# Norms transposed in pairs inside the projections of a two-layer transformer block, and four smaller moves

## The chip, the cores and the metric

The kernel runs on one core of a Trainium2 chip. The metric is the time of one execution on the device in microseconds. The engines are TensorE (PE: matmuls and transposes; PEld: its weight loads), VectorE (DVE), ScalarE (ACT), GpSimd (POOL) and SyncE (SP, which here only issues DMAs). DMAs are issued by SP, by ScalarE and by GpSimd, each in its own queue.

## What is computed

Two layers, with the same weights, over x of 2048 rows by 512 columns, all in float32:

```python
for _ in range(2):
    x = x + attention(layernorm(x), wqkv, wo)      # 32 heads of 16
    x = x + mish_mlp(layernorm(x), w1, b1, w2)     # 512 -> 1792 -> 512

# attention: softmax(q @ k.T * 16 ** -0.5) @ v, heads joined, then @ wo
# mish_mlp:  h = n @ w1 + b1;  (h * tanh(softplus(h))) @ w2
```

## The kernel before, in words

**Precision.** Every matmul of weights and activations is done as three: each operand is split into a high part, a rounded copy, and a low part, the difference, and `mm3` (L157) adds high x high, high x low and low x high. A projection step over 512 contraction rows is 4 blocks (k = 0 to 3) of 3 matmuls, 12 in all. `split_psum` (L153) splits a PSUM accumulator: ScalarE writes the high part, VectorE subtracts it from the accumulator for the low part. `split_load` (L109) loads a weight block; its inner `split` has ScalarE write the high part and GpSimd the low part.

**Stages of a layer.** The rows are cut into NCH = 4 chunks of 512; a chunk is 4 tiles of 128 rows.

1. Norm of each chunk (`norm_parts`, L164, a generator that gives the work out in parts): statistics of 4 tiles on VectorE (L175, L176), the power -1/2 on GpSimd (L172), the normalized tile `xn` on VectorE (L188), 4 transposes on TensorE (L199) for each tile, and the split into `th` and `tl` (L200). A chunk's `th` and `tl` are needed whole by the first projection step that reads it.
2. Projections (`qkv`, L446): a list `order` of steps (m, c), m = 0 to 3 for q and 4 to 7 for k, c the chunk. Each step accumulates in one of three PSUM accumulators (tag "s"), is split into a tile `pt` and written by a DMA that ScalarE issues (L479) to a scratch tensor `scr[m]` in DRAM. Once the eight steps with m in (0, 4) are done, `prep_qk(0)` reads the q and k rows of the first head group back: 2 pairs u by 2 heads e, each 7 transfers (one of ones, three of k, three of q), 28 in all, e = 0 on SP and e = 1 on GpSimd (L248). Later steps are followed by the first row maxima (`some_max`). Then v is projected (`v_parts`, L500).
3. Attention (`Attention.run`, L395), the longest stage: an order of scores, maxima and products written out by hand. It is not touched.
4. Output projection (`wo_parts`, called as `project`, L727). Between its blocks of three matmuls, the parts of the first norm for the hidden layer are placed by a table of block numbers (L741).
5. Hidden layer (`mlp`, L589): for each chunk c and each of FT = 14 blocks f, `hid` does the matmuls, ScalarE and VectorE the mish, with two products on GpSimd (L608, L611), and `outp`, two blocks later, the second matmul. The norms of the following chunk, and in layer 0 the norms of chunks 0 to 2 for layer 1, are spread over its blocks (`spread`, L207). The last norm for layer 1 is done inside `qkv` when chunk 3 is first needed (`late`, L462).

**What sets the order.** The kernel is written in program order; a planner then orders each engine's instructions by its own estimate of when each is ready, with three exceptions. `behind` (L100) pins an instruction behind the one written before it on the same engine. `att.pe` (L228) chains TensorE instructions in the order written, but only when `att.chained` is set, before the change only after `prep_qk(0)` (L489). DMA queues and engines then run in the order planned, each instruction waiting in its turn.

**Buffers.** Tag "f" has 2 buffers of 512 columns; it holds `xn`, the mish's `hb` and the attention's output tile `ot`. Tag "raw" has 3 buffers of 1024 columns; it holds raw weights and every second `pt`. Tag "ah" has 2, for the mish. Tag "mx" has 2 pairs of PSUM banks.

**Before the projections of layer 0**, L666 to L677 load chunk 0 of x, two weight blocks and the other chunks, and write out the norms of all four chunks; the planner mixes their transposes among the first steps.

Of the kernel before, what the change touches and what calls it, by code (L numbers as in the profile page):

```python
# [18 lines left out]
P = 128  # L19
S, D, H, DH, F = 2048, 512, 32, 16, 1792  # L20
NCH = 4
# [21 lines left out]
KEEP = 2  # L43
GSTEPS = NCH * NKT
# [9 lines left out]
def kernel(ctx: ExitStack, tc: tile.TileContext, x, wqkv, wo, w1, b1, w2, out):  # L54
# [20 lines left out]
    nc.sync.dma_start(b1t, b1.rearrange("(f p) -> p f", p=P))  # L75
# [33 lines left out]
    def split_load(key, src, a, b, later, raw=None):  # L109
        t = b8([P, 2, a, b], F32R, "s" + key)  # L110
        if raw is None:
            raw = tmp.tile([P, a, b], F32, tag="raw", name="r" + key, bufs=3)
        behind(nc.sync.dma_start(raw, src))

        def split():
            behind(nc.scalar.activation(t[:, 0], raw, AF.Copy))
            behind(nc.gpsimd.tensor_tensor(t[:, 1], raw, t[:, 0].bitcast(F32), op=ALU.subtract))
            unkept.append((key, t))

        later.append(split)  # L120
        return t
# [42 lines left out]
    def norm_parts(src, nm, got, key, tag, fine=False, pin=lambda ins: ins, pe=lambda ins: ins, halves=False):  # L164
# [20 lines left out]
        for t in range(NCH):  # L185
            xn = t512("f", f"xn{nm}{t}")
            pin(
                nc.vector.tensor_scalar(  # L188
                    xn, src[:, t], mv[:, t, 0:1], rs[:, t : t + 1], op0=ALU.subtract, op1=ALU.mult
                )  # L190
            )
            if halves:
                yield
            if tag == "mx":
                tp = ps.tile([P, 2, 512], F32, tag=tag, name=f"tp{nm}{t}")[:, 0]
            else:
                tp = pbank(tag, f"tp{nm}{t}")
            for k in range(KT):
                pe(nc.tensor.transpose(tp[:, ts(k, P)], xn[:, ts(k, P)], ident))  # L199
# [3 lines left out]
    def norm(src, nm, got, key, tag, fine=False):  # L203
        for _ in norm_parts(src, nm, got, key, tag, fine):
            pass
# [6 lines left out]
    class Attention:  # L212
# [26 lines left out]
        def prep_qk(self, g):  # L239
            l = self.l  # L240
            ks, qs = [], []
            for u in range(HG // 2):
# [3 lines left out]
                for e in range(2):  # L246
                    r0 = e * HALF
                    queue = nc.gpsimd if g == 0 and e else nc.sync  # L248
                    queue.dma_start(
                        k[r0 + KROWS : r0 + MROWS].bitcast(F32).rearrange("p (r n) -> p r n", n=P),  # L250
                        ones[:, None, :].to_broadcast([MROWS - KROWS, S // P, P]),
                    )
                    yield
                    for t, parts, base in ((k, K_PARTS, NCH), (q, Q_PARTS, 0)):
                        for j, a in enumerate(parts):
                            queue.dma_start(
                                t[r0 + j * DH : r0 + (j + 1) * DH].bitcast(F32),
                                self.scr[base + m][a, (h0 + e) * DH : (h0 + e + 1) * DH, :].bitcast(F32),
                            )
                            yield  # L260
# [172 lines left out]
    def load_qkv(l, wts, which, later):  # L433
        raw = None
        for j in which:
# [3 lines left out]
            elif j < 4:  # L439
                wts[j] = split_load(key, *cols(wqkv, j), later)  # L440
# [5 lines left out]
    def qkv(l, wts, tt, order, late, due):  # L446
        scr = [dram.tile([2, P, S], F32R, name=f"scr{l}{m}") for m in range(2 * NCH)]
        att = Attention(l, scr)
# [10 lines left out]
        spare = []  # L459
        for n, (m, c) in enumerate(order):  # L460
            if c not in tt:
                late()  # L462
# [6 lines left out]
            else:  # L469
# [3 lines left out]
            mm3(  # L473
                acc,
                [(w[:, 0, k, ts(m % 2, P)], w[:, 1, k, ts(m % 2, P)], th[:, k], tl[:, k]) for k in range(KT)],
                pe=att.pe,
            )
# [4 lines left out]
            for fn in due.get((m, c), []):  # L482
                fn()
            if m in (0, 4):
                done += 1
                if done == 2 * NCH:
                    for _ in att.prep_qk(0):
                        pass
                    att.chained = True  # L489
# [8 lines left out]
        return att  # L498
# [90 lines left out]
    def mlp(l, x2s, w1t, w2t, tts, dst, hooks):  # L589
        acts, obs = {}, {}  # L590

        def hid(c, f):
# [15 lines left out]
            nc.gpsimd.tensor_tensor(hb, hb, e, op=ALU.mult)  # L608
            ah, al = t512("ah", "ah" + nm, F32R), t512("al", "al" + nm, F32R)
            nc.vector.tensor_tensor(ah, hb, r, op=ALU.mult)  # L610
            nc.gpsimd.tensor_tensor(hb, hb, r, op=ALU.mult)  # L611
# [43 lines left out]
    wts, tt, late = {}, {}, None  # L655
# [11 lines left out]
    load_qkv(0, wts, (0, 2), splits)  # L667
    xc.append(load_x(1))
    for c in range(NCH):
        parts = norm_parts(xc[c], f"q0{c}", tt, c, "mx", c == 0)  # L670
        next(parts)
        if c == 0:
            split_all(splits)
        for _ in parts:
            pass
        if c + 2 < NCH:
            xc.append(load_x(c + 2))  # L677
    for l in range(2):
        due = {}
        if l == 0:  # L680
# [8 lines left out]
        att = qkv(l, wts, tt, order, late, due)  # L689
# [90 lines left out]
        if l == 0:  # L780
            late = lambda: norm(x2s[last], f"q1{last}", tt, last, "mx", True)
# [29 lines left out]
```

## Time and profile before

| | |
|---|---|
| time of the runs, median of 3 (lowest to highest) | 3623.95 us (3623.9 to 3626.84) |
| the profiled execution's own time | 3625.2 us |
| its span, first to last instruction | 3623.4 us |
| mean granted TensorE clock | 0.997 |
| attention, layer 0 (100 to 1455 us, with the end of its projections): TensorE busy | 1345.1 of 1355 us |
| attention, layer 1 (1900 to 3258 us): TensorE busy | 1347.8 of 1358 us |

Lines of a profile name an engine, a line of the kernel (L199), an operation and the tiles it writes and reads, as out<-in. In a view in order of time, a line begins with start and duration in microseconds, "x4" joins four instructions, and the bracket says how long the engine stood idle before and who released it. In a view of waits, a line has the waiting instruction, the one it waited for, and total, number and longest in microseconds. "ACTq" or "SPq" is a DMA being issued on that engine's queue.

### The profile page before, as it was taken

How to read it: one execution, taken by the hardware profiler on the slowest of the kernel's cores; microseconds unless marked ns; L12 is line 12 of the kernel's file. 1: busy time of each engine (PE TensorE's matmuls, PEld its weight loads, DVE VectorE, ACT ScalarE, POOL GpSimd, SP SyncE). 2: the span in 40 equal slices, each digit the busy share in tenths (PEclk: the TensorE clock that was granted, in tenths of full speed). 3: DMA queues.
4: the chain of work that ended last, by engine and by line, in shares of the span. 5: the costliest groups of instructions: out<-in, count | busy, mean ns of one | idle time of the engine just before them, and what ended most of it. 6: DMA issues, size and time to landing. Idle time of an engine off the chain costs nothing. (4 is left out here: it accounts for less than half of the span.)

```text
span 3623.4 us, 69472 instructions
## 1 busy us (share of the span) xinstructions
PE 3553.0 (98%) x28784; PEld 1948.5 (54%) x28784; DVE 2963.7 (82%) x2978; ACT 2520.7 (70%) x3475; POOL 567.6 (16%) x589
## 2 busy tenths in 40 slices
PE   7999999999999999999999999999999999999999
PEld 5644444444444444777776444444444444447887
DVE  4779999999999994666647799999999999946565
ACT  2178888888888888344421788888888888873444
POOL 2200101001000002345421000000000000024455
PEclk9999999999999999999999999999999999999999
DMA  6551313313122224600164311112021211245000
GB/s 192 202 157 38 79 49 69 68 40 78 48 51 60 51 78 65 183 35 12 47 197 150 66 31 35 36 40 43 19 46 28 46 33 33 78 69 179 36 12 24
DMA packets 128707, 254.07 MB, mean 70 GB/s; under 512 B 18680, under 2 KB 62584, under 8 KB 114568
## 3 DMA queue, kind: packets, MB, share of 16 engines
q1 hardware_dynamic: 101896, 174.58, 19.8%
q0 software_dynamic: 8224, 35.21, 3.5%
q10 hardware_dynamic: 18272, 39.85, 3.0%
q8 instruction: 226, 3.70, 0.4%
q14 instruction: 89, 0.73, 0.1%
HBM read 148.38 MB, written 99.09 MB: 68 GB/s over the span
## 5 line engine op out<-in xcount | busy, mean ns | idle before, releaser
L297 DVE TENSOR_REDUCE mxv<-pm 128x2 f32<-128x1024 f32 x2048 | 2388.0, 1219 | 180.7 <-PE pm L293 132.7
L348 ACT ACTIVATE p<-sp 128x1024 f32<-128x1024 f32 x1366 | 1396.9, 1023 | 17.5 <-PE sp L347 12.3
L373 PE MATMUL pv<-p,va 128*32 128x128 f32 (+3 forms) x16048 | 1166.9, 392 | 0.0
L293 PE MATMUL pm<-ks,qs 48*128 48x512 f32 x4096 | 1106.8, 445 | 0.2
L358 ACT ACTIVATE p<-ss 128x512 f32<-128x512 f32 x1364 | 815.2, 598 | 384.7 <-PE ss L357 290.3
L347 PE MATMUL sp<-qs,ks 50*128 50x512 f32 x2732 | 737.8, 447 | 4.5 <-ACT p L348 2.2
L293 PEld LDWEIGHTS pm<-ks,qs 48*128 48x128 f32 x4096 | 460.0, 184 | 360.6 <-issue 256.8
L373 PEld LDWEIGHTS pv<-p,va 128*32 128x32 f32 x16048 | 368.2, 108 | 498.2 <-issue 417.8
L357 PE MATMUL ss<-qs,ks 50*128 50x512 f32 x1364 | 610.7, 448 | 0.1
L357 PEld LDWEIGHTS ss<-qs,ks 50*128 50x128 f32 x1364 | 252.0, 185 | 305.3 <-ACT p L358 210.6
L347 PEld LDWEIGHTS sp<-qs,ks 50*128 50x128 f32 x2732 | 276.7, 183 | 202.3 <-ACT p L348 117.3
L320 POOL CAST np<-nf 16x128 fp32r<-16x128 f32 x64 | 17.9, 280 | 2230.5 <-ACT nf L319 2188.2
L608 POOL TENSOR_TENSOR hb<-hb,he 128x512 f32<-128x512 f32 x112 | 157.6, 1407 | 188.2 <-DVE he L605 184.1
L611 POOL TENSOR_TENSOR hb<-hb,hr 128x512 f32<-128x512 f32 x112 | 160.4, 1432 | 137.3 <-DVE ah L610 129.5
L612 DVE TENSOR_TENSOR al<-hb,ah 128x512 fp32r<-128x512 f32 x112 | 108.0, 964 | 84.5 <-POOL hb L611 82.2
L606 ACT ACTIVATE hr<-he 128x512 f32<-128x512 f32 x112 | 70.8, 632 | 151.6 <-POOL hb L611 77.0
L154 ACT ACTIVATE pt<-qk 128x512 fp32r<-128x512 f32 x64 | 37.9, 598 | 158.9 <-PE qk L162 127.5
L604 ACT ACTIVATE he<-he 128x512 f32<-128x512 f32 x112 | 70.8, 632 | 102.9 <-DVE he L603 99.7
L602 ACT ACTIVATE hb<-h,b1t 128x512 f32<-128x512 f32 x112 | 76.8, 685 | 77.2 <-DVE al L612 52.0
L610 DVE TENSOR_TENSOR ah<-hb,hr 128x512 fp32r<-128x512 f32 x112 | 76.9, 687 | 61.4 <-ACT hr L607 34.3
L605 DVE SCALAR_TENSOR_TENSOR he<-he 128x512 f32<-128x512 f32 x112 | 79.9, 714 | 41.9 <-ACT he L604 39.1
L603 DVE TENSOR_SCALAR he<-hb 128x512 f32<-128x512 f32 x112 | 68.0, 608 | 48.5 <-POOL hb L608 33.9
(225 smaller groups left out, 3277.7 us busy)
## 6 DMA issues: line engine op xcount, KB each, us to landing
scr<-pt ACTq DMA_DIRECT2D x64, 512.0 KB
qs<-scr SPq DMA_DIRECT2D x180, 128.0 KB
ks<-scr SPq DMA_DIRECT2D x180, 128.0 KB
vscr<-v SPq DMA_DIRECT2D x32, 512.0 KB
va<-vscr SPq DMA_DIRECT2D x64, 256.0 KB
oscr<-ot SPq DMA_DIRECT2D x64, 256.0 KB
ww<-sw POOLq DMA_DIRECT2D x14, 1024.0 KB, 5.2
qs<-np SPq DMA_DIRECT2D x512, 2.0 KB
```

The source lines that it names most:

```text
L293: nc.tensor.matmul(pm[:, e], qs[u][rows, q0 : q0 + P], ks[u][rows, ts(n, 512)], start=True, stop=True)
L297: nc.vector.tensor_reduce(self.mxs[b][:, 2 * u : 2 * u + 2, qt, n], pm, axis=AX.X, op=ALU.max)
L347: self.pe(nc.tensor.matmul(sp[:, e], k, q, start=True, stop=True))
L348: nc.scalar.activation(self.pts[-1][:, 0:n], sp[:, 0:n], AF.Exp, scale=SCALE)
L357: self.pe(nc.tensor.matmul(sp, k, q, start=True, stop=True))
L358: nc.scalar.activation(self.pts[i // 3][:, 2], sp, AF.Exp, scale=SCALE)
L373: nc.tensor.matmul(self.accs[b][ts(h, VW), cols], self.va[b // NCH][:, kt, h, :], self.pts[j][:, e, cols], start=kt == 0 and q0 == 0, stop ...
L605: nc.vector.scalar_tensor_tensor(e, e, 2.0, e, op0=ALU.add, op1=ALU.mult)
L608: nc.gpsimd.tensor_tensor(hb, hb, e, op=ALU.mult)
L610: nc.vector.tensor_tensor(ah, hb, r, op=ALU.mult)
L611: nc.gpsimd.tensor_tensor(hb, hb, r, op=ALU.mult)
L612: nc.vector.tensor_tensor(al, hb, ah.bitcast(F32), op=ALU.subtract)
```

## The change

1. `norm_parts` for tag "mx": four `xn` are made at once, in buffers of "f" and "ah"; two tiles are transposed into both banks of a pair, and split by one ScalarE and one VectorE instruction of 1024 columns. These norms are pinned (`behind`) and chained (`att.pe`).
2. `qkv` takes a table `within`: at block k of step n it goes on with a norm. In layer 0 the statistics and `xn` of chunks 1, 2, 3 are written at the start of steps 0, 3, 6, their transposes before blocks 1 and 3 of steps 2, 5, 7. In layer 1 the last norm's parts stand at step 4 and at blocks 0 and 2 of step 9, and the step (5, 1) is moved ahead of (0, 3). `att.chained` is set from the first instruction on.
3. `prep_qk(0)`: the 14 transfers of the second pair (u = 1) are issued by ScalarE, pinned, two after each later step; of the first pair 7 are on SP and 7 on GpSimd.
4. The low halves of the first two weight blocks are formed by VectorE, not GpSimd. The load of the bias b1 moves from the head of SP's queue behind the loads of x.
5. Norms spread over the hidden layer (tag "acc") take `xn` from "raw" instead of "f". The table of block numbers in the output projections changes. In the last two blocks of the last chunk, the mish's two products are done by VectorE instead of GpSimd.

```diff
+PREP = 7
...
-    def split_load(key, src, a, b, later, raw=None):
+    def split_load(key, src, a, b, later, raw=None, low=nc.gpsimd):
...
-            behind(nc.gpsimd.tensor_tensor(t[:, 1], raw, t[:, 0].bitcast(F32), op=ALU.subtract))
+            behind(low.tensor_tensor(t[:, 1], raw, t[:, 0].bitcast(F32), op=ALU.subtract))
...
-        for t in range(NCH):
-            xn = t512("f", f"xn{nm}{t}")
+        def scaled(t, tag):
+            if tag == "raw":
+                xn = tmp.tile([P, 2, 512], F32, tag=tag, name=f"xn{nm}{t}", bufs=3)[:, 0]
+            else:
+                xn = t512(tag, f"xn{nm}{t}")
...
+        if tag == "mx":
+            xns = [scaled(t, ("f", "ah")[t // 2]) for t in range(NCH)]
+            yield
+            for u in range(NCH // 2):
+                tp = ps.tile([P, 2, 512], F32, tag=tag, name=f"tp{nm}{u}")
+                for e in range(2):
+                    for k in range(KT):
+                        pe(nc.tensor.transpose(tp[:, e, ts(k, P)], xns[2 * u + e][:, ts(k, P)], ident))
+                two = ts(u, 2 * P)
+                split_psum(
+                    th[:, :, two].rearrange("p k (t n) -> p k t n", n=P),
+                    tl[:, :, two].rearrange("p k (t n) -> p k t n", n=P),
+                    tp.rearrange("p t (k n) -> p k t n", n=P),
+                    pin,
+                )
+                yield
+            return
+        for t in range(NCH):
+            xn = scaled(t, "raw" if tag == "acc" else "f")
...
-                    queue = nc.gpsimd if g == 0 and e else nc.sync
+                    queue = nc.sync
+                    pin = lambda ins: ins
+                    if g == 0 and u:
+                        queue, pin = nc.scalar, behind
+                    elif g == 0 and e:
+                        queue = nc.gpsimd
...
-            if c not in tt:
-                late()
+            for fn in within.get((n, 0), []):
+                fn()
...
+            for k in range(KT):
+                for fn in within.get((n, k), []) if k else []:
+                    fn()
+                mm3(
+                    acc,
+                    [(w[:, 0, k, ts(m % 2, P)], w[:, 1, k, ts(m % 2, P)], th[:, k], tl[:, k])],
+                    first=k == 0,
+                    last=k == KT - 1,
+                    pe=att.pe,
+                )
...
+            for _ in range(2):
+                next(parts, None)
             if m in (0, 4):
                 done += 1
                 if done == 2 * NCH:
-                    for _ in att.prep_qk(0):
-                        pass
-                    att.chained = True
+                    parts = att.prep_qk(0)
+                    for _ in range(2 * PREP):
+                        next(parts)
...
-            nc.gpsimd.tensor_tensor(hb, hb, e, op=ALU.mult)
+            mul = nc.vector if (l, c) == (1, NCH - 1) and f >= FT - 2 else nc.gpsimd
+            mul.tensor_tensor(hb, hb, e, op=ALU.mult)
...
-            nc.gpsimd.tensor_tensor(hb, hb, r, op=ALU.mult)
+            mul.tensor_tensor(hb, hb, r, op=ALU.mult)
...
-    load_qkv(0, wts, (0, 2), splits)
-    xc.append(load_x(1))
-    for c in range(NCH):
-        parts = norm_parts(xc[c], f"q0{c}", tt, c, "mx", c == 0)
...
+    load_qkv(0, wts, (0, 2), splits, nc.vector)
+    xc += [load_x(c) for c in range(1, NCH)]
+    nc.sync.dma_start(b1t, b1.rearrange("(f p) -> p f", p=P))
+    att = attention(0)
+    att.chained = True
+    norms = [norm_parts(xc[c], f"q0{c}", tt, c, "mx", c == 0, behind, att.pe) for c in range(NCH)]
+    for i in range(4):
+        next(norms[0])
+        if i > 1:
+            splits.pop(0)()
...
+            for c, (n0, n1) in enumerate(((0, 2), (3, 5), (6, 7)), 1):
+                for at in ((n0, 0), (n0, 0), (n1, 1), (n1, 3)):
+                    within.setdefault(at, []).append(lambda c=c: next(norms[c]))
...
-            order = [(0, 0), (0, 1), (0, 2), (4, 0), (4, 1), (4, 2), (1, 0), (1, 1), (1, 2), (5, 0), (0, 3), (4, 3)]
+            order = [(0, 0), (0, 1), (0, 2), (4, 0), (4, 1), (4, 2), (1, 0), (1, 1), (1, 2), (5, 0), (5, 1), (0, 3), (4, 3)]
+            att = attention(1)
+            att.chained = True
+            late = norm_parts(x2s[NCH - 1], f"q1{NCH - 1}", tt, NCH - 1, "mx", True, pe=att.pe)
+            for at in ((4, 0), (4, 0), (9, 0), (9, 2)):
+                within.setdefault(at, []).append(lambda: next(late))
...
-            for n in range({0: 1, 6: 1, 9: 2, 12: 2, 15: 2}.get(i, 0)):
+            for n in range({0: 1, 8: 1, 11: 2, 14: 2}.get(i, 0)):
                 next(first)
         for i, _ in enumerate(project(2)):
-            if i == 1:
+            for n in range({1: 2, 4: 1}.get(i, 0)):
                 next(first)
```

More of the change, by code (lines that the diff above doesn't have):

```diff
@@ L431, in run, with load_qkv @@
             open_banks()
-    def load_qkv(l, wts, which, later):
+    def load_qkv(l, wts, which, later, low=nc.gpsimd):
         raw = None
@@ L439, in load_qkv @@
             elif j < 4:
[L440 removed]
+                wts[j] = split_load(key, *cols(wqkv, j), later, low=low)
             else:
```

47 lines of the change are left out of this document (14 added, 33 removed).

## The prediction

> **What bounds the kernel now.** I read the page's head first, then busy time by stage (columns: stage, its length, then busy us and instructions of TensorE, its weight loads, VectorE, ScalarE, GpSimd; granted clock; DMA).
>
> ```profile
> span 3623.4 us, 69472 instructions
> PE 3553.0 (98%) x28784; PEld 1948.5 (54%) x28784; DVE 2963.7 (82%) x2978; ACT 2520.7 (70%) x3475; POOL 567.6 (16%) x589
> ```
>
> ```profile
> 8.83:100.00 91.17, 76.84 (x325) 61.12 (x326) 44.04 (x83) 26.45 (x43) 25.63 (x26) 0.94 0.65 208
> 1455.00:1482.00 27.00, 25.86 (x146) 18.67 (x145) 19.68 (x33) 3.00 (x5) 4.22 (x5) 1.00 0.67 186
> 1482.00:1750.00 268.00, 264.37 (x1177) 215.34 (x1176) 169.16 (x250) 121.62 (x188) 133.50 (x102) 1.00 0.17 58
> 1750.00:1832.00 82.00, 77.01 (x347) 59.70 (x345) 49.57 (x86) 39.21 (x63) 33.38 (x26) 1.00 0.23 84
> 1832.00:1900.00 68.00, 62.00 (x258) 50.12 (x260) 24.59 (x46) 13.96 (x25) 13.78 (x21) 0.92 0.70 211
> 3258.00:3282.00 24.00, 21.36 (x124) 15.42 (x121) 17.23 (x27) 2.99 (x5) 2.94 (x2) 1.00 0.67 177
> 3282.00:3612.00 330.00, 327.93 (x1461) 268.82 (x1460) 199.12 (x290) 152.37 (x235) 166.70 (x125) 1.00 0.15 53
> 3612.00:3618.50 6.50, 4.80 (x19) 2.99 (x17) 2.33 (x4) 1.35 (x2) 2.58 (x2) 1.00 0.00 0
> ```
>
> TensorE sets the time, so a change that leaves its work alone can win only its idle time and its time at a lower clock. Its idle time here is 14.3 us in the first projections, 6.0 in the second ones, 3.6, 5.0 and 2.1 in the hidden layers, 1.1 and 2.6 in the output projections, 1.7 at the tail: 36 us. At full clock a matmul costs 327.93/1461 = 0.225 us, so one step of the projections (12 matmuls) 2.7 us. Next I asked whom TensorE waits for (total, times, longest): the first five lines are from 8 to 100 us, the next three from 1832 to 1900, the last two from 1750 to 1832.
>
> ```profile
> PE tpq L199 <- DVE xnq L188: 8.8, 1, 8.8
> PE tpq L199 <- DVE tlq L155: 6.6, 3, 5.1
> PE qk L160 <- DVE pt L155: 4.0, 2, 3.1
> PE tpq L199 <- DVE mvq L176: 2.3, 1, 2.3
> PE qk L160 <- ACT thq L154: 1.4, 2, 0.7
> ...
> PE qk L160 <- DVE pt L155: 2.7, 1, 2.7
> PE tpq L199 <- DVE tlq L155: 2.0, 1, 2.0
> PE qk L160 <- ACT thq L154: 1.4, 2, 0.7
> ...
> PE mo L162 <- DVE al L612: 2.7, 3, 1.3
> PE h L160 <- ACT hb L602: 1.6, 5, 0.3
> ```
>
> The 8.8 is the wait for the first data. Last the clock (after the busy times):
>
> ```profile
> 37.60:44.40 6.80, 5.86 (x17) 4.71 (x18) 3.38 (x11) 0.64 (x2) 1.77 (x2) 0.50 0.03 5
> 85.40:88.70 3.30, 2.86 (x7) 2.28 (x8) 0.39 (x1) 2.47 (x4) 1.33 (x1) 0.50 1.01 137
> 1860.30:1867.10 6.80, 6.11 (x18) 4.84 (x19) 1.83 (x3) 1.19 (x2) 0.00 (x0) 0.50 0.21 80
> 1891.10:1894.40 3.30, 3.30 (x10) 2.52 (x9) 1.05 (x2) 0.60 (x1) 0.00 (x0) 0.50 1.06 303
> ```
>
> Behind each of the waits of 2.3, 3.1, 2.0 and 2.7 us stands a stretch at half clock; half its busy time is lost too: 2.9, 1.4, 3.1 and 1.65 us.
>
> **A, the start.** Views in order of time:
>
> ```profile
> 8.63 1.06 ACT L116 ACTIVATE sqkv<-rqkv 128x1024 fp32r<-128x1024 f32 x1 [6.60 <-DMA rqkv<-in_A_wqkv_dram]
> 8.83 1.97 PE L199 MATMUL tpq<-ident,xnq 128*128 128x128 f32 x8 [8.83 <-DVE xnq L188]
> 10.02 4.83 POOL L117 TENSOR_TENSOR sqkv<-rqkv,sqkv 128x1024 fp32r<-128x1024 f32 x2
> 10.07 5.07 DVE L188 TENSOR_SCALAR xnq<-x,mvq,rsq 128x512 f32<-128x512 f32 x2 [0.56 <-POOL rsq L172]
> 18.51 1.65 PE L160 MATMUL qk<-thq,sqkv 128*128 128x512 f32 x3 [0.69 <-ACT thq L154]
> 20.15 0.79 PE L161 MATMUL qk<-tlq,sqkv 128*128 128x512 f32 x1
> 1461.62 1.22 DVE L587 TENSOR_TENSOR x<-wo,x 128x1024 f32<-128x1024 f32 x1 [0.52 <-PE wo L162]
> ```
>
> While GpSimd forms the low halves of the weights (2.4 us each), two xn, normally about 0.5 us each, take 5.07, and the transposes behind them start 5.1 us late. The change gives these low halves to VectorE (1.2 us each by the 128x1024 row) and each xn a buffer of its own. If the transposes start at 8.8 again, 16 of them end at 12.8. ScalarE then does th, weight, th, weight at 1.06 each: the second th ends at 14.2. VectorE does tl, weight low, tl at 1.22: 12.05 + 3.7 = 15.7, where the second matmul starts, against 20.15 now, when three are done instead of one (two at half clock, 0.86 less). 20.15 - 15.7 - 0.86 = 3.6; the bias load no longer stands ahead of x on SP, which I estimate at half a microsecond, under the 0.8 of uncertainty. I take 4.0, bounds 3 and 5.
>
> **B, norms 1 to 3 inside the projections.** TensorE's order is now fixed, so a late xn holds everything queued behind its transpose: the remaining matmuls of the step. Before: 0.7 + 1.5 + 2.3 + 0.9 = 5.4 us of waits (the lines above without 8.8, 5.1, 3.1 and A's 0.7), and 2.9 at half clock: 8.3. After, from these rows:
>
> ```profile
> 20.11 2.43 DVE L175 BATCH_NORM_STATS2 stq<-x 128x6 f32<-128x512 f32 x4
> 22.69 2.10 POOL L172 TENSOR_TENSOR rsq<-veq,mhalf 128x4 f32<-128x4 f32 x2 [7.83 <-DVE mvq L176]
> 23.74 1.01 DVE L188 TENSOR_SCALAR xnq<-x,mvq,rsq 128x512 f32<-128x512 f32 x2 [0.65 <-POOL rsq L172]
> ```
>
> Norm 1 has its stats behind the weight halves and is wanted a whole step later: no wait. The stats of norm 2 are pinned behind the low half of step 2's eviction, which follows the second tl of norm 1. Its transposes end 0.7 us before step 2 does; then th 1.06, tl 1.22, that low half 0.7 and gaps bring VectorE to 2.5 us past the step. Stats 2.43, means and add 0.5, power 1.05 and a gap of 0.2, two xn 1.0: the first pair is ready at 7.7. TensorE wants it after two steps and three matmuls, 6.1: a wait of 1.6. Norm 3 stands so behind step 5, but is wanted after one step and three matmuls, 3.4: a wait of 4.3. It is over the 2.0 and 2.3 that were followed by half clock, so I add 1.4 to 3.1, say 2.2. Sum 8.1: B gains 0.2, bounds -4 (half clock also after the 1.6) and +8.3 (no wait at all).
>
> The Trainium skill ("TensorE: Matmul & The Clock Gate", Part 1) puts the clock's return to half at an idle window of about 3.4 us. By it only the 4.3 would bring half clock, as in my sum; the trace disagrees with it on size, since 2.0 us was enough here, and by that the 1.6 is close to costing 1.4 to 3.1 more.
>
> **C, the reads.** The first group's 28 transfers leave in one burst, 14 from SP and 14 from GpSimd.
>
> ```profile
> 70.19 1.38 SPq L256 DMA_DIRECT2D qs<-scr  x3
> 84.47 0.60 ACT L154 ACTIVATE pt<-qk 128x512 fp32r<-128x512 f32 x1 [9.23 <-DMA qs<-scr]
> ...
> ks<-scr POOLq DMA_DIRECT2D x6, 128.0 KB, 9.9
> ```
>
> ScalarE stood for 9.2 us until one of SP's reads had landed, though its next work, a write of pt and an eviction, uses none of that data; three accumulators later TensorE stood too (3.1, in layer 1 2.7). With 7 + 7 in the burst and the other 14 two per step, the queue halves. ScalarE pays 14 x 0.46 = 6.4 us per layer, 0.9 per step of 2.7 beside 0.6 eviction and 0.4 write: it lies beside matmuls. Before: 3.1 + 1.4 + 2.7 + 1.65 = 8.9. I take 8.0; bounds 0 and 8.9, and below nothing by the last rival.
>
> The Trainium skill ("DMA: Bandwidth & Descriptors", Issuing engines are not separate DMA queues) says that another issuing engine saves only issue time. By it C gives about nothing and the sum is 8 less; the 9.2 us wait speaks for more.
>
> **D, the late norm of layer 1.** Its transposes move to steps (5,0), with (5,1) between them and their user: 4.1 us of matmuls over th and tl, 2.3 plus gaps. Waits 2.0 + 1.4 and half clock 3.1 go: 6.5 at most (0.7 of the 1.4 may belong to the start of (0,2)); I take 5.5, bounds 3 and 6.5. VectorE's stats have four steps, 10.8 us, of cover.
>
> **E, hidden layers.** Spread norms take xn from "raw", not from "f", which holds hb in two buffers. The h and mo waits (1.6, 2.7) sit where xn holds one. I take 3 of 5.0 there, 2 of the 3.6 + 2.1 elsewhere: 5, bounds 0 and 9.
>
> **F, output projections.** xn and transposes come two blocks of three matmuls later, which is 1.4 us; the spacing between tiles stays. I take 1.5 of 3.7, bounds -1 and 3.
>
> **G, the tail.**
>
> ```profile
> 3613.49 0.69 DVE L610 TENSOR_TENSOR ah<-hb,hr 128x512 fp32r<-128x512 f32 x1 [1.57 <-POOL hb L608]
> 3614.24 0.50 PE L160 MATMUL mo<-w26l,ah 128*128 128x512 f32 x1 [0.75 <-DVE ah L610]
> 3616.32 0.50 PE L162 MATMUL mo<-w26l,al 128*128 128x512 f32 x1 [0.89 <-DVE al L612]
> ```
>
> Four products of 0.69 move from GpSimd (2.58/2 = 1.3 each) to VectorE. Both gaps, 1.64, shrink to about 0.25: 1.4, bounds 0.6 and 1.64.
>
> **Sum.** 4.0 + 0.2 + 8.0 + 5.5 + 5 + 1.5 + 1.4 = 25.6, from the profiled execution's own 3625.2 (span 3623.4 and 1.8 around it): 3599.6. That execution is 1.25 over the runs' median, so the runs should be at about 3598.
>
> **Rivals.** (1) Norms 2 and 3 come in time, because VectorE starts their stats before the evictions: B is 8.3, time 3590. The pinning speaks against it. (2) ScalarE's share brings nothing, since the same bytes saturate the DMA engines (share 1.01 at 85 us): 3606. (3) The removed waits come back: whatever TensorE gains in A it waits at the next fixed point, and D and E stand on another engine's latency; A, C and G alone halved, 6.7, give 3617. (4) Slower: a read on ScalarE holds the evictions behind it. If a step's pair waits for the pair before, and a read needs up to 9.9 us, a step takes 8 or more; seven steps lose 7 x (8 - 2.7) less the 4 us that three accumulators cover, 33 per layer, 66 in all, and C's 8 are gone: 3598 + 74 = 3672. It decides for slower once a step on ScalarE takes over 4.6 us (2 x (7 x 1.9 - 4) = 18.6, all the rest of the sum); half as many transfers in the burst speak against it.
>
> **Chances.** Forecast 0.62, its own range 3592 to 3604; (1) 0.13, (2) 0.11, (3) 0.07, (4) 0.07. Range 3586 (rival 1 with E's upper bound) to 3611 (rival 2 with B's lower one). A run of this kernel tells about 0.2%, 7.2 us: faster 0.86 (the forecast and rivals 1 and 2), same 0.07 (rival 3), slower 0.07 (rival 4).
>
> **What would show it.** A: GpSimd has no weight subtraction before 60 us, no xn over 0.6, dense matmuls from 15 to 16. B: the transposes of norm 3 wait some 4 us for xn, with half clock behind. C: no wait of ScalarE over 3 us, none of TensorE for pt. D: no wait at the late transposes, full clock through the second projections. E: no h wait for hb at the end of the first hidden layer. The prediction is wrong if ScalarE stands behind its own reads, or if TensorE's idle time before 100 us is over 20 us.

## The result, and the profile after

The changed kernel takes 3612.76 us (median of 13 runs, 3610.37 to 3617.14), the kernel before 3619.85 on the same chip (13 runs, 3616.01 to 3626.84). The ratio is 0.9978, with a 95% interval of 0.997 to 0.9987: it is faster by about 7 us. The prediction had 3598, with a range up to 3611; the gain is less than a third of the 25.6 us that were forecast. (The forecast stood on three runs at 3623.95 us, 4.1 above the median here; 25.6 off that median would be 3594.) The profiled execution takes 3617.14 us, 8.1 less than the one of before; the two are 5.4 and 4.4 us above their kernels' medians.

The head of the page after:

```profile
span 3615.0 us, 69442 instructions
...
PE 3558.0 (98%) x28784; PEld 1953.2 (54%) x28784; DVE 2967.4 (82%) x2974; ACT 2521.5 (70%) x3465; POOL 543.5 (15%) x569
```

TensorE is busy for 5 us *more* than before (3553.0) with the same number of instructions, in a span that is 8.4 shorter. So idle time went, and something else came. Busy time by stage says where; first the kernel before, cut at the stages' own ends (first projections, hidden layer 0, second projections, hidden layer 1), then the changed one with its stretches at half clock. Columns as in the prediction: stage, length, busy us and instructions of TensorE, its weight loads, VectorE, ScalarE, GpSimd; granted clock; DMA.

```profile
8.83:138.10 129.27, 114.94 (x494) 87.22 (x494) 75.39 (x114) 32.43 (x53) 31.06 (x29) 0.96 0.60 197
1486.70:1812.30 325.60, 318.69 (x1418) 257.23 (x1417) 205.50 (x311) 150.07 (x232) 156.51 (x118) 1.00 0.16 55
1815.80:1939.50 123.70, 116.32 (x502) 88.72 (x502) 66.86 (x97) 29.25 (x49) 27.77 (x30) 0.96 0.58 189
3290.30:3608.00 317.70, 315.63 (x1406) 258.74 (x1405) 191.75 (x275) 150.83 (x233) 161.99 (x119) 1.00 0.13 44
```

```profile
8.13:134.30 126.17, 114.85 (x494) 87.80 (x496) 74.01 (x105) 31.89 (x46) 22.05 (x18) 0.96 0.63 203
37.90:41.30 3.40, 3.40 (x14) 2.85 (x12) 1.23 (x1) 0.78 (x1) 0.00 (x0) 0.50 0.02 5
48.10:55.00 6.90, 4.84 (x17) 4.19 (x18) 3.31 (x6) 1.02 (x1) 1.77 (x2) 0.51 0.10 34
1484.00:1808.80 324.80, 323.26 (x1442) 263.13 (x1441) 212.78 (x321) 156.03 (x243) 161.57 (x122) 1.00 0.18 58
1811.80:1928.00 116.20, 111.39 (x479) 84.48 (x477) 59.40 (x81) 23.19 (x38) 19.16 (x19) 0.96 0.54 183
1826.50:1833.30 6.80, 6.13 (x14) 4.79 (x15) 4.29 (x15) 0.60 (x1) 2.79 (x5) 0.50 0.49 182
1894.70:1898.10 3.40, 3.40 (x9) 2.62 (x10) 2.20 (x3) 0.00 (x0) 0.00 (x0) 0.50 0.56 217
3278.10:3601.50 323.40, 320.34 (x1406) 259.53 (x1406) 190.73 (x275) 153.17 (x233) 154.80 (x118) 1.00 0.14 46
```

Three things stand out. The first projections are only 3.1 us shorter, and their clock is 0.96 as before: waits and half clock were exchanged for others. The second projections are 7.5 us shorter, though a new stretch at half clock (1826.5) stands at their start. And hidden layer 1 is 5.7 us *longer*: the same 1406 matmul records take 320.34 us instead of 315.63, at full clock. The matmuls themselves became slower.

By line (columns: busy us, mean ns of one; idle time before it), a matmul of the second product of hidden layer 1, before and after:

```profile
L160 PE MATMUL mo<-w24l,ah 128*128 128x512 f32 x32 | 12.5, 390 | 0.0
```

```profile
L160 PE MATMUL mo<-w24l,ah 128*128 128x512 f32 x32 | 12.7, 397 | 0.0
```

Matmuls overlap, so the 7 ns are read better from start to start: over all `mo` matmuls that follow one another without a wait, 227.7 and 227.2 ns in layers 0 and 1 before, 233.4 and 233.7 after. The `h` matmuls go from 227.6 and 227.1 to 228.3 and 228.6. A layer has 672 of each (4 chunks x 14 blocks x 12): 672 x 6.1 + 672 x 1.1 = 4.8 us per layer. The order of TensorE's instructions differs little, and nothing in the diff touches these matmuls, except one thing: `norm_parts` now takes its `xn` from "f" and "ah", so that the tag "ah" is first asked for right behind "f", ahead of the row maxima's small buffers and of "hr" and "he". Buffers are laid out in the order in which their tags first occur. By the sizes of the buffers, `ah` moves from byte 220928 of each partition to 214656; `al` stays at 225024. 220928 and 225024 are multiples of 256; 214656 is 128 beyond one.

The first projections: two lines of TensorE's waits from 8 to 100 us, then VectorE in order of time around norm 2.

```profile
PE tpq L205 <- DVE xnq L192: 15.5, 3, 8.1
PE qk L160 <- DVE pt L155: 1.8, 3, 1.1
```

```profile
27.98 1.22 DVE L155 TENSOR_TENSOR tlq<-tpq,thq 128x1024 fp32r<-128x1024 f32 x1 [0.82 <-ACT thq L154]
29.12 0.68 DVE L155 TENSOR_TENSOR pt<-qk,pt 128x512 fp32r<-128x512 f32 x1
29.72 0.68 DVE L175 BATCH_NORM_STATS2 stq<-x 128x6 f32<-128x512 f32 x1
31.11 0.68 DVE L155 TENSOR_TENSOR pt<-qk,pt 128x512 fp32r<-128x512 f32 x1
...
33.69 0.69 DVE L155 TENSOR_TENSOR pt<-qk,pt 128x512 fp32r<-128x512 f32 x1 [0.44 <-ACT pt L154]
34.50 0.17 DVE L171 TENSOR_SCALAR veq<-mvq 128x4 f32<-128x4 f32 x1
35.86 1.92 DVE L192 TENSOR_SCALAR xnq<-x,mvq,rsq 128x512 f32<-128x512 f32 x4 [1.19 <-POOL rsq L172]
```

Of the 15.5, 8.1 is the start; the rest is 2.85 us before norm 2's transposes and 4.55 before norm 3's, where 1.6 and 4.3 were forecast. From the first statistics (29.72) to the first `xn` (35.86) VectorE needs 6.1 us and not 4.2: the low halves of two evictions (31.11 and 33.69) were placed between the statistics, each 0.7, with 0.44 of waiting. Behind both waits stands half clock.

### The profile page after: what moved, and what is told of

Same layout as the page of the kernel before. It is cut to its first block, busy times and chain, and to the rows that moved or that the text cites. A ratio compares the mean times of both kernels' runs of the same rounds, so it can differ in the third digit from the quotient of the medians.

```text
span 3615.0 us, 69442 instructions
## 1 busy us (share of the span) xinstructions
PE 3558.0 (98%) x28784; PEld 1953.2 (54%) x28784; DVE 2967.4 (82%) x2974; ACT 2521.5 (70%) x3465; POOL 543.5 (15%) x569
## 4 chain that ended last, share of the span: by engine, by line
PE 87%; DVE 3%; ACT 3%; DMA 2%; issue 2%; POOL 1%; ACTq 0%; SPq 0%; DVEq 0%; POOLq 0%
PE pv L396 29%; PE pm L316 17%; PE ss L380 12%; PE sp L370 9%; PE mo L162 2%; PE mo L160 2%; PE mo L161 2%; PE h L160 2%; PE h L161 2%; PE h L162 2%; ACT p L381 1%; PE qk L160 1%; PE qk L161 1%; PE qk L162 1%; POOL hb L644 1%
## 5 line engine op out<-in xcount | busy, mean ns | idle before, releaser
L641 POOL TENSOR_TENSOR hb<-hb,he 128x512 f32<-128x512 f32 x110 | 150.0, 1364 | 193.0 <-DVE he L637 189.2
L644 POOL TENSOR_TENSOR hb<-hb,hr 128x512 f32<-128x512 f32 x110 | 154.7, 1406 | 127.1 <-DVE ah L643 116.0
L645 DVE TENSOR_TENSOR al<-hb,ah 128x512 fp32r<-128x512 f32 x112 | 95.8, 856 | 61.6 <-POOL hb L644 61.4
L635 DVE TENSOR_SCALAR he<-hb 128x512 f32<-128x512 f32 x112 | 78.1, 697 | 47.9 <-ACT hb L634 34.4
```

What stands on the lines that cost most here:

```text
L641: mul.tensor_tensor(hb, hb, e, op=ALU.mult)
L644: mul.tensor_tensor(hb, hb, r, op=ALU.mult)
```

## The experiments

Each time stands with its ratio to the kernel before, run beside it on the same chip; the changed kernel itself is 0.9978. "Changed" in a label means that all else is as in the changed kernel.

### Where ah stands

Unused allocations at the head of the tmp buffers fix the order of the tags. In the first two runs each kernel gets the other's places. The edit of the first is below; the list of the second ends with "ah" right behind "f".

```diff
+    for tag, shape, dt, bufs in (
+        ("raw", [P, KT, 2 * P], F32, 3),
...
+        ("f", [P, 512], F32, 2),
+        ("mxv", [P, HG, NCH, NCH], F32, 2),
...
+        ("hr", [P, 512], F32, 1),
+        ("he", [P, 512], F32, 1),
+    ):
+        tmp.tile(shape, dt, tag=tag, name="first" + tag, bufs=bufs)
```

> The changed kernel, instruction for instruction; only the places of its work buffers in SBUF are those of the kernel before (the mish's high part ah, 214656 bytes from the start of a partition, goes back to 220928, its partners with it). Theory 'places': the second matmul of the hidden layer (mo) was slowed from 227 to 234 ns by where its operands lie; it returns to 227, each hidden layer is some 5 us shorter, the kernel some 10 us: ratio about 0.995 to the kernel before (now 0.998). Rival 'other engines': the slower mo comes from what runs beside it, which is the same here; mo stays at 234 and the time does not move.

> The kernel before, instruction for instruction, with its work buffers at the changed kernel's places. Theory 'places': mo goes from 227 to 234 ns, each hidden layer is some 5 us longer, the kernel some 10 us: ratio about 1.003. Rival 'other engines': mo stays at 227, ratio 1.000.

With the old places the changed kernel takes 3605.13 us, 0.9953 (0.9941 to 0.9966); with the new places the kernel before takes 3623.99, 1.0008 (0.9999 to 1.0017). In the traces each engine has the same instructions as in the kernel it is made from, in the hidden layers in the same order. The matmuls followed the places in both (table below). So the places cost the changed kernel about 9 us by the ratios. In the profiled executions its hidden layers get 2.6 and 3.3 us shorter, 6 of the 9.6 that the slower matmuls make. In the kernel before less than expected shows of it: its hidden layers grow by 1.2 and 2.3 us. Its TensorE is busy there for 3.1 and 3.6 us longer, but without work for 1.9 and 1.3 us less: part of the slowness lies in time that was waited anyway.

Four more runs ask which property of the place counts. In order: 128 unused bytes ahead of `ah`, with `al` right behind it; 128 bytes ahead of `ah` in the old order; `ah` and `al` ahead of nearly all else; 64 bytes ahead of `ah` in the old order.

```diff
 # changed_aligned_new_place
         ("f", [P, 512], F32, 2),
+        ("pada", [P, 32], F32, 1),
+        ("ah", [P, 512], F32, 2),
+        ("al", [P, 512], F32, 2),
 # changed_old_places_shifted; changed_ah_shifted_64 with [P, 16]
         ("he", [P, 512], F32, 1),
+        ("pada", [P, 32], F32, 1),
 # changed_ah_at_512
         ("raw", [P, KT, 2 * P], F32, 3),
+        ("nm", [P, HG * NCH], F32, 2),
+        ("pad", [P, 32], F32, 1),
+        ("ah", [P, 512], F32, 2),
+        ("al", [P, 512], F32, 2),
```

> Instructions as in the changed kernel; 128 unused bytes stand ahead of ah, and al follows ah, so that both begin at a multiple of 256 bytes per partition, but at 214784 and 218880, where they are in neither kernel; hr and he stand at 128 beyond a multiple. If the slow matmul comes from ah's offset within 256 bytes (128 in the changed kernel, 0 before), mo goes back to 227 to 228 ns and the ratio to 0.995 to 0.996. If it comes from the neighbourhood of ah and f, or from the distance between ah and al, mo stays at 233 ns and the ratio at 0.998.

> Instructions as in the changed kernel, tmp buffers in the order of the kernel before, but 128 unused bytes ahead of ah: ah at 221056 and al at 225152, both 128 beyond a multiple of 256 bytes, all else where it was before. If the offset within 256 bytes decides, mo is at 233 ns or more and the ratio at 0.998 again; if the order of the buffers decides, mo stays at 227 to 228 ns and the ratio at 0.995.

> Instructions as in the changed kernel; ah begins at 210432 and al at 214528, multiples of 512 bytes (so far the fast places were 256 beyond a multiple of 512, the slow ones 128 beyond). If a multiple of 256 is what counts, mo stands at 227 to 228 ns and the ratio at 0.995 to 0.996. If just the place 256 beyond 512 is fast, mo is at 233 ns and the ratio at 0.998.

> Instructions as in the changed kernel, buffers in the order of the kernel before, 64 unused bytes ahead of ah: ah at 220992 and al at 225088, 64 beyond a multiple of 256. If any offset from 256 is slow, mo is at 233 ns or more and the ratio at 0.9975 or above, as with 128. If only an offset of 128 is slow, mo is at 227 to 228 ns and the ratio 0.995.

| run | ah, al begin at byte | beyond a multiple of 256 | mo, ns from start to start (layers 0, 1) | hidden layers, first to last start of an h matmul, us | ratio (interval) |
|---|---|---|---|---|---|
| before | 220928, 225024 | 0, 0 | 227.7, 227.2 | 325.2, 317.3 | 1 |
| changed | 214656, 225024 | 128, 0 | 233.4, 233.7 | 324.4, 323.0 | 0.9978 (0.997 to 0.9987) |
| changed_old_places | 220928, 225024 | 0, 0 | 227.8, 227.5 | 321.8, 319.6 | 0.9953 (0.9941 to 0.9966) |
| before_new_places | 214656, 225024 | 128, 0 | 233.5, 233.7 | 326.4, 319.6 | 1.0008 (0.9999 to 1.0017) |
| changed_aligned_new_place | 214784, 218880 | 0, 0 | 227.8, 227.7 | 321.8, 319.8 | 0.9958 (0.9945 to 0.997) |
| changed_ah_at_512 | 210432, 214528 | 0, 0 | 227.8, 227.7 | 321.3, 319.9 | 0.9952 (0.9934 to 0.997) |
| changed_old_places_shifted | 221056, 225152 | 128, 128 | 233.1, 233.0 | 324.3, 323.0 | 0.9976 (0.9967 to 0.9986) |
| changed_ah_shifted_64 | 220992, 225088 | 64, 64 | 233.2, 233.2 | 324.4, 323.0 | 0.9974 (0.9962 to 0.9986) |

The same group of matmuls as above, by line (the unused allocations shift the line numbers), in changed_aligned_new_place and in changed_old_places_shifted:

```profile
L173 PE MATMUL mo<-w24l,ah 128*128 128x512 f32 x32 | 12.4, 389 | 0.0
```

```profile
L177 PE MATMUL mo<-w24l,ah 128*128 128x512 f32 x32 | 12.7, 396 | 0.0
```

Neither the neighbours nor the region decide: `ah` is fast at three different places that are multiples of 256 bytes, and slow at three that are not, one of them only 64 bytes from a fast one. Offsets other than 0, 64 and 128 were not tried. By which path the offset costs time stays open. Slices of `ah` and `al` are the stationary operands here. In the changed kernel even two successive matmuls on `al`, which had not moved, stand at 232 to 233 ns, so it isn't simply the load of a misplaced operand ahead of its own matmul.

### xn in "raw"

Part of E undone: the spread norms take `xn` from "f" again.

```diff
-            xn = scaled(t, "raw" if tag == "acc" else "f")
+            xn = scaled(t, "f")
```

> The changed kernel with the xn of the norms spread over the hidden layers in tag f again (part 5 of the change undone there), at the changed kernel's places. Theory 'places': mo stays at 234; the waits of h for hb and of mo for al come back, some 5 us: 5 us slower than the changed kernel, ratio about 0.9995. Rival 'the new xn buffer slows the hidden layer': mo returns to 227 and the kernel gets faster, ratio about 0.996.

3615.69 us, 0.9983 (0.9974 to 0.9992): less than expected. The difference from the changed kernel, 2 us, is well inside the intervals, so that "raw" may be worth nothing. In the profiled execution TensorE waits for `hb` again in hidden layer 0, 1.8 us; that stage is 1.8 us longer, layer 1 1.3 shorter. The `mo` matmuls stay at 233.4 and 233.6 ns.

### Statistics one step earlier

```diff
-            for c, (n0, n1) in enumerate(((0, 2), (3, 5), (6, 7)), 1):
-                for at in ((n0, 0), (n0, 0), (n1, 1), (n1, 3)):
+            for c, (ns, n0, n1) in enumerate(((0, 0, 2), (2, 3, 5), (5, 6, 7)), 1):
+                for at in ((ns, 0), (n0, 0), (n1, 1), (n1, 3)):
```

> The changed kernel with the statistics of norms 2 and 3 in layer 0 written at steps 2 and 5 instead of 3 and 6 (their xn stay). Theory 'pinned behind the eviction': the waits of 2.9 and 4.6 us of TensorE for xn shrink to under 1 us each and the two stretches at half clock (3.4 and 6.8 us) go: the first projections are 8 to 11 us shorter, ratio about 0.9955. Rival 'VectorE is simply full there': the waits stay within 1 us of what they were, ratio 0.998.

3600.6 us, 0.9942 (0.9929 to 0.9954): 13 us below the changed kernel by the ratios. TensorE's waits from 8 to 100 us, then its busy time from 20 to 100 us:

```profile
PE tpq L205 <- DVE xnq L192: 8.9, 2, 8.5
```

```profile
20.00:100.00 80.00, 77.18 (x360) 60.31 (x359) 45.27 (x70) 23.85 (x34) 18.12 (x16) 1.00 0.69 214
```

All but 0.4 us of the wait for `xn` beside the start is gone, and from 20 us on the clock is 1.00: the two waits and what followed them were the loss of part B. The first projections end at 123.3 us; in the nine executions that have those of the changed kernel they end at 131.3 to 134.3, so 8 to 11 of the 13 us stand there.

### The reads in one burst

Part C undone: 14 reads from SP and 14 from GpSimd at once.

```diff
-                    if g == 0 and u:
-                        queue, pin = nc.scalar, behind
-                    elif g == 0 and e:
+                    if g == 0 and e:
                         queue = nc.gpsimd
...
-                    for _ in range(2 * PREP):
-                        next(parts)
+                    for _ in parts:
+                        pass
```

> The changed kernel with part C undone: all 28 reads of the first group leave at once, 14 from SP and 14 from GpSimd. Theory: ScalarE stands again behind the reads for 9 us, TensorE waits some 3 us for pt in each layer with a stretch at half clock behind it, and the time goes up by 6 to 9 us, to 3619 to 3622 (ratio 1.000). Rival, that ScalarE's share brings nothing: TensorE's wait for pt stays under 1 us and the ratio at 0.998.

3621.61 us, 0.9998 (0.9989 to 1.0007): the time is that of the kernel before, so C is worth about 7 us. ScalarE and then TensorE in layer 1, in order of time:

```profile
1867.61 0.60 ACT L154 ACTIVATE pt<-qk 128x512 fp32r<-128x512 f32 x1 [3.98 <-DMA qs<-scr]
1883.27 0.37 ACTq L508 DMA_DIRECT2D scr<-pt  x1
1883.74 0.60 ACT L154 ACTIVATE pt<-qk 128x512 fp32r<-128x512 f32 x1 [15.53 <-DMA scr<-pt]
```

```profile
1885.12 0.80 PE L160 MATMUL qk<-thq,qkv1l 128*128 128x512 f32 x1 [11.24 <-DVE pt L155]
```

VectorE has the tile ready for ScalarE's next write at 1868.9; the write is issued at 1883.3, and the eviction behind it has waited 15.5 us. All three accumulators fill, and TensorE stands for 11.2. In layer 0 the waits for `pt` came back too (2.0 and 1.6 us, this time without half clock behind them). The first projections end only 0.2 us later than in the profiled execution of the changed kernel, but 1.8 to 3.1 later than in three others with stretches at half clock in the same places (changed_xn_in_f, changed_old_places_shifted, changed_old_places).

### The weights' low halves on GpSimd

```diff
-    load_qkv(0, wts, (0, 2), splits, nc.vector)
+    load_qkv(0, wts, (0, 2), splits)
```

> The changed kernel with this piece of part A undone: GpSimd, not VectorE, forms the low halves of the first two weight blocks. Prediction's step: xn beside GpSimd takes 2.5 us each again, the first matmul starts some 5 us later, and the time goes up by about 4 us, to 3617 (ratio 0.999). Rival, that what is won at the start is waited for again at the pinned norms 2 and 3: the start is later by 4 to 5 us, but the first projections end no more than 1.5 us later, and the ratio stays at 0.998.

3611.4 us, 0.9971 (0.9959 to 0.9984): nothing is lost, so neither description was right. The start, in order of time:

```profile
7.90 1.91 DVE L192 TENSOR_SCALAR xnq<-x,mvq,rsq 128x512 f32<-128x512 f32 x4
...
12.55 4.70 POOL L117 TENSOR_TENSOR sqkv<-rqkv,sqkv 128x1024 fp32r<-128x1024 f32 x2 [3.61 <-ACT sqkv L116]
13.44 0.80 PE L160 MATMUL qk<-thq,sqkv 128*128 128x512 f32 x1 [1.26 <-ACT thq L154]
14.70 0.80 PE L161 MATMUL qk<-tlq,sqkv 128*128 128x512 f32 x1 [0.46 <-DVE tlq L155]
```

GpSimd now starts at 12.55, when the four `xn` are long done: it waits for the weight's high half, which ScalarE in the pinned order forms behind the first `th`. So the change of engine was not what freed `xn`. The pinned order is enough by this trace; the buffers that `xn` got in the same edit were not tried apart from it.

### The late norm of layer 1

Part D undone: the norm is written where chunk 3 is first used, the step (5, 1) is back in its place, and TensorE's order is free until the reads.

```diff
                     parts = att.prep_qk(0)
+                    att.chained = True
...
-            order = [..., (5, 0), (5, 1), (0, 3), (4, 3)]
+            order = [..., (5, 0), (0, 3), (4, 3)]
             att = attention(1)
-            att.chained = True
-            late = norm_parts(x2s[NCH - 1], f"q1{NCH - 1}", tt, NCH - 1, "mx", True, pe=att.pe)
-            for at in ((4, 0), (4, 0), (9, 0), (9, 2)):
+            late = norm_parts(x2s[NCH - 1], f"q1{NCH - 1}", tt, NCH - 1, "mx", True)
+            for at in 4 * [(10, 0)]:
```

> The changed kernel with part D undone: in layer 1 the last norm is written where chunk 3 is first used, the step (5, 1) stands where it stood, and TensorE's order is free until the reads. Prediction's step: waits of 3.4 us and a stretch at half clock come back at the late transposes, 5.5 us, to 3618 (ratio 0.9993). Rival from the changed kernel's trace, where a new wait of 2.6 us with 6.8 us at half clock stands at the start of layer 1: that wait is the price of the fixed order and goes with it, so the balance is 0 to 2 us (ratio 0.998).

3612.81 us, 0.9974 (0.9963 to 0.9985): the time of the changed kernel. TensorE's waits from 1810 to 1900 us with D undone:

```profile
PE qk L160 <- ACT thq L154: 3.3, 2, 2.5
PE qk L160 <- DVE pt L155: 1.1, 1, 1.1
```

One wait of 2.5 us stands where the changed kernel has 2.6 elsewhere, at the start of the layer:

```profile
1823.47 0.60 PE L221 MATMUL tpq<-ident,xnq 128*128 128x128 f32 x4
1824.80 0.49 PE L160 MATMUL qk<-thq,qkv0l 128*128 128x512 f32 x1 [0.74 <-ACT thq L154]
1825.84 0.67 DVE L155 TENSOR_TENSOR pt<-qk,pt 128x512 fp32r<-128x512 f32 x1
1826.43 0.68 DVE L155 TENSOR_TENSOR tlq<-tpq,thq 128x512 fp32r<-128x512 f32 x1
1827.17 0.79 PE L161 MATMUL qk<-tlq,qkv0l 128*128 128x512 f32 x1 [1.87 <-DVE tlq L155]
```

The last transposes for chunk 2 end at 1824.1, right ahead of the step (0, 2) that needs them. Their split goes through ScalarE and VectorE, behind the low half of an eviction, and TensorE's fixed order offers nothing else in the meantime. 6.8 us at half clock follow; of the ten profiled executions with this wait three have 6.8 us, six 3.4 and one none.

### Chunk 2 two steps later

```diff
-            order = [(0, 0), (0, 1), (0, 2), (4, 0), (4, 1), (4, 2), ...]
+            order = [(0, 0), (0, 1), (4, 0), (4, 1), (0, 2), (4, 2), ...]
```

> The changed kernel, but in layer 1 the steps (4, 0) and (4, 1) come ahead of (0, 2), so that chunk 2 is first used two steps later. If the wait at the start of layer 1 is what takes D's gain back, TensorE waits under 0.5 us for chunk 2's th and tl, there is no half clock between 1810 and 1840, and 4 to 6 us are won: 3607 to 3609, ratio 0.9965. If the last transposes for chunk 2 are only planned later too, or the same time is waited at the reads (1.2 and 0.8 us stand there now), the ratio stays at 0.998.

3605.82 us, 0.9955 (0.9942 to 0.9967): 8 us below the changed kernel by the ratios, more than expected. The longest wait of TensorE from 1790 to 1900 us is now one of 1.1 us for an eviction, and the second projections run at full clock. They take 107.8 us; in nine executions that have those of the changed kernel they take 112.2 to 116.2, so 4 to 8 us stand in the stage itself:

```profile
PE qk L160 <- DVE pt L155: 1.1, 1, 1.1
```

```profile
1810.00:1917.80 107.80, 106.47 (x479) 81.30 (x479) 59.00 (x81) 23.32 (x39) 19.36 (x19) 1.00 0.60 198
```

### Two faults, and all three, undone

The first run joins the edits of changed_early_stats and changed_old_places, the second those two and that of changed_chunk2_later.

> The changed kernel with both of its faults undone at once: the statistics of norms 2 and 3 written one step earlier, and the tmp buffers at the places that they had before. If the two are independent (waits of TensorE in the first projections; a slower second matmul in the hidden layers), the gains add: 0.9978 for the changed kernel, 0.0036 less for the early statistics, 0.0025 less for the places: ratio 0.9917, about 3590 us. If the waits of one hide in the other, the ratio stays at 0.994. TensorE's wait for xn before 100 us under 1 us beside the start, the mo matmuls at 227 to 228 ns from start to start.

> The same order of steps on the version with early statistics and the buffers at their old places (0.9927). There the wait at the start of layer 1 is 2.6 us with 3.4 us at half clock behind it, 4.3 us in all: 3590 us, ratio 0.9915, if it is won; 0.9927 if it is waited for at the reads.

Early statistics with the old places: 3594.58 us, 0.9927 (0.9915 to 0.994). Of the 0.0061 that the two gains make together, 0.0051 is there: they lie in different stages. With chunk 2 later as well: 3589.32 us, 0.991 (0.9894 to 0.9925), the fastest version, some 25 us below the changed kernel by the ratios. Its head:

```profile
span 3586.0 us, 69442 instructions
...
PE 3538.5 (99%) x28784; PEld 1943.4 (54%) x28784; DVE 2967.1 (83%) x2974; ACT 2520.6 (70%) x3465; POOL 545.3 (15%) x569
```

## Why the prediction was too low

The prediction's sum, regrouped by stage, beside the profiled executions (before less after, from first and last instructions of each stage):

| stage | terms | forecast gain, us | measured |
|---|---|---|---|
| start and first projections | A 4.0, B 0.2, half of C 4.0 | 8.2 | 3.9 |
| both attentions | none | 0 | -3.1 |
| output projections | F | 1.5 | 2.6 |
| hidden layers, to the next projections | E | 5 | -4.4 |
| second projections | half of C 4.0, D 5.5 | 9.5 | 7.5 |
| tail | G | 1.4 | 2.0 |
| sum | | 25.6 | 8.5 (the spans: 8.4) |

These are one execution each. The hidden layers come out the same within 0.7 us wherever another run repeats their instructions at the same offset, but for one of 1.9. The projections do not: before_new_places, with the instructions of the kernel before, ends the first ones at 133.2 us and not 138.1, and its second ones take 121.1 and not 123.8. So the measured gains of the two projection stages are known to some 5 us only.

**The step that failed is E**, and with it the assumption that an edit changes only waits. It came out at -4.4, outside its bounds of 0 and 9, and is 9.4 of the 17 us that the sum is short. The prediction asked where `xn` holds a buffer, and not where the new allocation puts the others. The waits for `hb` and most of those for `al` did go: from 1486.7 and 1484.0 on, hidden layer 0 had 6.9 us without TensorE before (325.60 less 318.69) and 1.5 after. But 4.8 us per layer, 9.6 in all, went into slower matmuls. With the places put back, hidden layer 0 gains 3.4 us and layer 1 loses 2.3 against before, 1.1 together where 5 were forecast. The loss of layer 1 stands in waits that are new: TensorE waits there 2.7 us for `al` and 1.1 for `ah`, where before it was 1.1 for `al` and 0.7 for `thm`. So E's own gain was put too high as well; why `ah` and `al` come later in layer 1 isn't settled.

The Trainium skill ("SBUF — State Buffer", SBUF: two separate sides) names the port that VectorE and GpSimd share, and DMA's own ports, as the only places of contention, and says that TensorE's port waits for no one. Nothing there lets the byte at which an operand begins change a matmul's time. Here it did, by 6 ns in 227, in both directions; so that rule can't be used to hold a matmul's time constant over a new allocation.

**B was the right mechanism, mis-sized.** It forecast waits of 1.6 and 4.3 and 2.2 at half clock, 8.1 in all. Measured: 2.85 and 4.55, and half of 3.40 and of 4.84 busy us at half clock, 1.7 and 2.4; 11.5 in all. B is then 8.3 less 11.5, a loss of 3.2, near the lower bound of 4 that the prediction gave for half clock after the first wait too. What it had wrong is VectorE's queue: it put the statistics behind one eviction, and two more came between them. The run with early statistics shows rival 1 as a remedy: without these waits the first projections end 14.9 us earlier than before, not 3.9 (9.9 and -1.1 against before_new_places).

The Trainium skill ("TensorE: Matmul & The Clock Gate", Part 1) has the clock fall after an idle window of about 3.4 us. The trace disagrees on the size once more: 2.85 us was followed by half clock, and so, in most executions, were 0.74 and 1.87 us with one matmul between them.

**A was near in size, for the execution it was taken from, and wrong in its reason.** From the start of the changed kernel:

```profile
11.19 1.22 DVE L155 TENSOR_TENSOR tlq<-tpq,thq 128x1024 fp32r<-128x1024 f32 x1 [1.75 <-ACT thq L154]
14.73 0.80 PE L161 MATMUL qk<-tlq,sqkv 128*128 128x512 f32 x1 [0.87 <-DVE tlq L155]
```

The second matmul starts at 14.73 us where 15.7 was forecast, 20.15 before: by the prediction's working 20.15 - 14.73 - 0.86 = 4.6, where 4.0 was taken. Against the execution of before_new_places, where it starts at 18.14, it is 2.6, under the lower bound of 3: the size was in part that of one execution. And the engine of the low halves has no part in it, as its run shows.

**C held.** 8.0 were forecast; undone, it costs 7 us by the ratio. The signs that were named for it did not come out: ScalarE still stands up to 7.0 us in layer 1. Its waits there from 1850 to 1900 us, one line:

```profile
ACT pt L154 <- DMA ks<-scr: 12.1, 2, 7.0
```

In these 7.0 us it issues two of its own reads, the write of `pt` only behind them (at 1875.1; the tile was ready at 1871.3) and two more reads, and only then does the next eviction. So rival 4, reads on ScalarE that hold up the evictions, did begin, and the prediction had named that as a sign of being wrong. (Its other sign, over 20 us without TensorE before 100 us, stayed away: 19.4.) But the three accumulators covered nearly all of it: TensorE waits 0.8 us for `pt` in layer 1 and 1.8 in layer 0. Of the stretches at half clock that C was to remove, the one of layer 1 stayed (1894.7 to 1898.1).

**D was given back.** Its waits and the half clock at 1860 are gone, as forecast, but the fixed order set a new wait of 2.6 us at the start of the layer, mostly with 3.4 or 6.8 us at half clock behind it. That is rival 3 in one stage. Undoing D changes nothing that the intervals tell; taking the new wait away wins 8 us by the ratios and 4 to 8 in the stage. What the stage gained all the same, 7.5 us, is mostly C's: with the burst it takes 122.1 us.

**F and G** came out 1.1 and 0.6 better than forecast. **The attentions** were to be untouched, and lost 1.6 and 1.5 us. In the run with the reads in a burst, layer 0 lost nothing and layer 1 1.0; in the other runs made from the changed kernel layer 0 lost 0.7 to 1.9, and layer 1 between -0.4 and 1.0. How much of it is more than a difference between executions stays open.

## What to carry to other kernels

Before costing an edit that adds, drops or first uses a buffer elsewhere, compare the bytes at which the matmuls' operands begin in both versions; here 64 or 128 bytes off a multiple of 256 cost a stream of matmuls 2.6%, and an unused allocation got it back. Where TensorE's order is fixed by hand, cost each fixed point by the whole queue of the engine that feeds it, other stages' evictions included, and put the producer's first instruction a step earlier than the sum asks. Count a wait of 2.3 us or more in a dense stream at 1.4 to 3.1 us above its length, for the half clock that stood behind each of them here. And when one execution is profiled, ask of a second one which of its waits come back, before a forecast is built on their sizes.

## What the runs showed of the hardware that was not expected

- A matmul's spacing depends on where its operands begin: 227 to 228 ns with `ah` and `al` at multiples of 256 bytes, 233 to 234 ns with `ah`, or both, 64 or 128 bytes beyond, over more than 1100 pairs of matmuls in each of eight runs. The `h` matmuls beside them, whose own operands did not move, slow by about 1 ns too.
- Half clock comes in stretches of 3.4 us or several in a row: 6.8, and 10.2 around the wait of 11.2 us in changed_reads_in_burst. In the 16 profiled executions, from 22 us on, all 30 waits of TensorE of 2.3 us or more have such a stretch in them or right behind them, and 11 of 15 waits of 1.6 to 2.1 us; of 40 waits of 1.0 to 1.5 us one has.
- Which it is differs between executions of the same instructions. The 1.99 us wait at the late transposes has 6.8 us at half clock behind it in the kernel before and none in before_new_places. The start differs too: the matmuls of the first steps stand 427 ns apart up to 20.5 us in the changed kernel, and only up to 17.7 in changed_old_places; the first projections end at 134.3 and 131.3.
- With 28 reads in one burst, ScalarE stood for 15.5 us behind a single write in layer 1, and for 9.2 us in layer 0 of the kernel before, with the tile to be written ready 14.3 and 8.0 us before the write was issued.
